# A SwiGLU layer on one core: the first loads of a kernel move between three issuing queues

## The chip, the core and the metric

The kernel runs on one core of one Trainium2 chip. A core has TensorE (PE in the profile, its weight loads PEld), VectorE (DVE), ScalarE (ACT), GpSimd (POOL) and SyncE (SP). SP does no arithmetic; it issues DMAs. The metric is the device time of one execution in microseconds (us); of the kernel before there are three runs. A profile of one more execution gives a span, from the first to the last instruction, and the times of all instructions and DMAs, counted here from the start of the span.

## What is computed

x has 2048 tokens of 512 values, and the hidden width F is 1376 (10 tiles of 128 columns and one of 96); all inputs are bf16.

```python
g = silu(x @ w_gate)      # x: 1 x 2048 x 512, w_gate: 512 x 1376
u = x @ w_up              # w_up: 512 x 1376
out = (g * u) @ w_down    # w_down: 1376 x 512
```

## The kernel before

TensorE works through a list of groups written out in the program (`groups`). A group G or U is 128 columns of F (a tile `ft`) of the gate or up product for 512 tokens (a chunk `c`): four steps over the depth of 512 (`dk`), each of two matmuls of 64 columns of F that run side by side in the array, into one of eight PSUM banks. ScalarE takes the silu of a gate out of its bank, VectorE multiplies it by the up product into `hT_sb`. After four chunks of this, and of the 96 columns that are left (groups X and Y), the same array computes the output from `hT_sb` and w_down in groups of four 32-row strips (`strips`, L456) and at the end in whole rows (`whole_rows`, L433). TensorE waits for a load the first time that it uses it (`need`).

The contraction runs over x's depth, so x is needed with depth on partitions (`xT_sb`). Tokens 256 and up are transposed by DMA (`load_x`, L93). The first 256 tokens come as they are into `xn_sb` (L114), and TensorE transposes them with an identity matrix (L374, L382), which GpSimd's iota (L274) and VectorE (L299) make; VectorE and ScalarE copy the result into `xT_sb` (L309, L291). Until `xn` has landed, TensorE runs matmuls on constants whose results nobody reads: `N_WARM` of 512 columns (L359), and `N_FILL` pairs of 128 columns with half the rows each (L364).

The order of the first useful work is written out by hand at L385 to L394: for tiles 0 and 1, gates and ups of tokens 0 to 255 (32 matmuls of 256 columns), then tile 0's gate of tokens 256 to 383 and of 384 to 511 (8 matmuls of 128 columns each), then the other three groups of tokens 256 to 511 (24 matmuls of 256 columns). The next groups are the gates of tiles 2 and 3 and their ups, with 512 tokens at once, and so on.

The loads that the change touches, with the name of each one's semaphore:

- `xn`: tokens 0 to 255; `x0b` and `x0c`: tokens 256 to 383 and 384 to 511, transposed.
- `wg0`, `wu0`: gate and up weights of tiles 0 and 1 (256 KB each); `wg2`, `wu2`: of tiles 2 and 3; `wg4`, `wu4` and so on in the same way (`slabs`).

Each engine's DMA instructions go through that engine in program order. Before, `wg0` is the first instruction of ScalarE (`loads_on_scalar`, L110). All the others are SP's (`loads_on_sync`, L113): xn, wu0, x0b, x0c, wg2, wu2, wg4, wu4 and on. GpSimd issues no DMA.

Of the kernel before, what the change touches and what calls it, by code (L numbers as in the profile page):

```python
# [6 lines left out]
BF16 = mybir.dt.bfloat16  # L7
FP32 = mybir.dt.float32

N_WARM = 6  # L10
N_FILL = 2


def bass_standalone__swiglu_ffn__prompt_kernel(nc, x, w_gate, w_up, w_down, out):
    _, S, D = x.shape
    F = w_gate.shape[1]
    P = 128
# [24 lines left out]
    UPH = F + 32  # L42
# [4 lines left out]
    with ExitStack() as es:  # L47
# [33 lines left out]
        loads = {}  # L81

        def load_sem(name):
            loads[name] = sem(f"s_{name}")
            return loads[name]
# [6 lines left out]
        def load_x(eng, name, t0, t1):  # L92
            eng.dma_start_transpose(  # L93
                xT_sb[:, :, t0:t1], xf[t0:t1, :]
            ).then_inc(load_sem(name), 16)

        def load_w(eng, name, src, base, f0, f1):
            eng.dma_start(
                w_sb[:, :, base + f0:base + f1],
                src[:, f0:f1].rearrange("(k p) f -> p k f", p=P),  # L100
            ).then_inc(load_sem(name), 16)

        slabs = [(0, 2), (2, 4), (4, 6), (6, 8), (8, NFT)]
        slab_of = {ft: a for a, b in slabs for ft in range(a, b)}

        def load_slab(eng, a, b):
            load_w(eng, f"wg{a}", w_gate, 0, a * P, min(b * P, F))
            load_w(eng, f"wu{a}", w_up, UPH, a * P, min(b * P, F - 32))

        def loads_on_scalar(act):  # L110
            load_w(act, "wg0", w_gate, 0, 0, slabs[0][1] * P)

        def loads_on_sync(sp):  # L113
            sp.dma_start(  # L114
                xn_sb[:, :, :].rearrange("p j d -> p (j d)"), xf[0:HT, :].rearrange("(p j) d -> p (j d)", j=NXN)
            ).then_inc(load_sem("xn"), 16)
            load_w(sp, "wu0", w_up, UPH, 0, slabs[0][1] * P)
            load_x(sp, "x0b", HT, HT + P)
            load_x(sp, "x0c", HT + P, SC)
            for a, b in slabs[1:]:  # L120
                load_slab(sp, a, b)
            load_w(sp, "wut", w_up, F - (F - 32), F - 32, F)
            for c in range(1, NSC):
                load_x(sp, f"x{c}", c * SC, (c + 1) * SC)
            sp.dma_start(
                wd_sb[:, 0:NFF, :], w_down[0:NFF * P, :].rearrange("(k p) d -> p k d", p=P)
            ).then_inc(load_sem("wd"), 16)
            for c in range(NSC):
                sp.dma_start(
                    wdt_sb[R * c:R * (c + 1), :, :], w_down[NFF * P:F, :].rearrange("(q p) d -> p q d", p=R)  # L130
                ).then_inc(load_sem(f"wdt{c}"), 16)
            sp.dma_start(wdl_sb[:, :], w_down[NFF * P:F, LASTA:D]).then_inc(load_sem("wdl"), 16)
# [86 lines left out]
        for dk in range(KD):  # L219
            g = add_group("T", dk=dk)  # L220
            eng = "DA"[dk % 2]
# [19 lines left out]
        for at in range(NST):  # L241
# [4 lines left out]
            for c0, c1 in [(0, LASTA), (LASTA, LASTB), (LASTB, D)] if end else [(0, D)]:  # L246
                g = add_group("O", t=t, c0=c0, c1=c1, c=c)
                (quads[j] if c0 == 0 else last).append(g)
                eng = "A" if (end and c0 == 0) or (j < TPC - 1 and c % 2) else "D"
                op = add_op(  # L250
                    eng, g, kind="copy", out=o_sb[ob][:, c0:c1], src=g["bank"][:, 0:c1 - c0],
# [6 lines left out]
        def rows_of(t):  # L258
            if t < NXN:
                return of[0:HT, :].rearrange("(p j) d -> j p d", j=NXN)[t]  # L260
            return of[t * P:(t + 1) * P, :]

        def on_sync(sp):
            loads_on_sync(sp)
            for t, c0, c1, ob, eng, n in stores:
                if (c0, c1) == (0, LASTA):
                    continue
                sp.wait_ge(s_A if eng == "A" else s_D, n)
                sp.dma_start(rows_of(t)[:, c0:c1], o_sb[ob][:, c0:c1]).then_inc(s_out[ob], 16)
            for i in range(NST, NST + NOS):  # L270
                sp.wait_ge(s_out[i % NOS], 16 * n_store[i % NOS])

        def on_gpsimd(pool):
            pool.iota(  # L274
                diag[:, :], pattern=[[-1, P]], base=0, channel_multiplier=1,
            ).then_inc(s_I, 1)

        def on_scalar(act):
            loads_on_scalar(act)
            act.activation(adummy[:, 0:4], zero_c, ACT.Silu)  # L280
            for op in act_ops:
                act.wait_ge(s_P, op["g"]["at"] + 1)
                if op["kind"] == "silu":
                    if op["free"]:
                        act.wait_ge(s_D, op["free"])
                    fn = ACT.Silu
                else:
                    if op["stored"][1]:
                        act.wait_ge(*op["stored"])
                    fn = ACT.Copy  # L290
                act.activation(op["out"], op["src"], fn).then_inc(s_A, 1)  # L291
            for t, c0, c1, ob, eng, n in stores:
                if (c0, c1) == (0, LASTA):
                    act.wait_ge(s_A, n)
                    act.dma_start(rows_of(t)[:, c0:c1], o_sb[ob][:, c0:c1]).then_inc(s_out[ob], 16)
# [16 lines left out]
        def on_tensor(pe):  # L312
# [44 lines left out]
            def warm(n, width):  # L357
                for i in range(n):
                    pe.matmul(banks[NB - 1][:, 0:width], lhsT=ones_w, rhs=ones_m[:, 0:width], start=True, stop=True)  # L359

            warm(N_WARM, SC)
            for i in range(N_FILL):
                for h in range(2):
# [147 lines left out]
                ).then_inc(s_P, 1)  # L511

        on_sync(nc.sync)
        on_gpsimd(nc.gpsimd)
        on_scalar(nc.scalar)
        on_tensor(nc.tensor)
        on_vector(nc.vector)

# [27 lines left out]
```

## Time and profile before

| What | us |
|---|---|
| runs (three) | 120.25, 119.51, 119.60; median 119.6 |
| profiled execution | 120.67 |
| its span | 119.3 |
| PE busy | 116.6 (98%) |
| DVE, ACT busy | 43.4, 35.5 |
| POOL busy | 0.4 |
| matmuls of L345 (gate and up) | 71.0 in 680 |
| matmuls of L456, L433 (output) | 26.9 in 480, 8.7 in 59 |

The profiled execution is 1.37 us longer than its span, and 1.07 us longer than the median of the runs. The records of a few matmuls are missing from a trace like this. "Idle" of TensorE can be hidden in its busy time, since the ends of matmuls are modelled; the starts are measured.

### The profile page before, as it was taken

How to read it: one execution, taken by the hardware profiler on the slowest of the kernel's cores; microseconds unless marked ns; L12 is line 12 of the kernel's file. 1: busy time of each engine (PE TensorE's matmuls, PEld its weight loads, DVE VectorE, ACT ScalarE, POOL GpSimd, SP SyncE). 2: the span in 40 equal slices, each digit the busy share in tenths (PEclk: the TensorE clock that was granted, in tenths of full speed). 3: DMA queues.
4: the chain of work that ended last, by engine and by line, in shares of the span. 5: the costliest groups of instructions: out<-in, count | busy, mean ns of one | idle time of the engine just before them, and what ended most of it. 6: DMA issues, size and time to landing. Idle time of an engine off the chain costs nothing.

```text
span 119.3 us, 2992 instructions
## 1 busy us (share of the span) xinstructions
PE 116.6 (98%) x1343; PEld 66.4 (56%) x1344; DVE 43.4 (36%) x68; ACT 35.5 (30%) x61; POOL 0.4 (0%) x5
## 2 busy tenths in 40 slices
PE   7999999999999999999999999999999999999993
PEld 2796555555555555555555555554444444464452
DVE  0103534442534452444352444369800040214331
ACT  4225243265242365232454323470000030213001
POOL 1000000000000000000000000000000000000000
DMA  3999999991000000000000000000000023023612
GB/s 80 278 283 335 194 253 228 269 295 23 0 5 0 0 0 0 5 0 5 0 5 0 0 0 0 5 0 0 5 0 5 0 86 95 0 92 106 204 44 88
DMA packets 17596, 8.92 MB, mean 75 GB/s; under 512 B 8624, under 2 KB 17456, under 8 KB 17584
## 3 DMA queue, kind: packets, MB, share of 16 engines
q1 hardware_dynamic: 16912, 8.38, 27.1%
q10 hardware_dynamic: 672, 0.36, 1.0%
q8 instruction: 10, 0.16, 0.6%
q14 instruction: 2, 0.02, 0.0%
HBM read 4.81 MB, written 2.10 MB: 58 GB/s over the span
## 4 chain that ended last, share of the span: by engine, by line
PE 98%; issue 0%; DVE 0%
PE psum L345 59%; PE psum L456 24%; PE psum L433 7%; PE psum L409 3%; PE psum L359 2%; PE psum L420 1%; PE psum L382 0%; PE psum L374 0%; PE psum L364 0%; DVE o_sb L309 0%; PE psum L508 0%
## 5 line engine op out<-in xcount | busy, mean ns | idle before, releaser
L345 PE MATMUL psum<-xT_sb,w_sb 128*64 128x512 bf16 (+2 forms) x680 | 71.0, 371 | 0.0
L345 PEld LDWEIGHTS psum<-xT_sb,w_sb 128*64 128x64 bf16 x680 | 43.0, 112 | 27.1
L305 DVE TENSOR_TENSOR hT_sb<-sg_sb,psum 128x512 bf16<-128x512 f32 x40 | 27.5, 687 | 41.5 <-PE psum L345 36.6
L291 ACT ACTIVATE sg_sb<-psum 128x512 f32<-128x512 f32 x40 | 23.8, 596 | 41.6 <-PE psum L345 41.6
L456 PE MATMUL psum<-wd_sb,hT_sb 32*128 32x512 bf16 x480 | 26.9, 374 | 0.0
L456 PEld LDWEIGHTS psum<-wd_sb,hT_sb 32*128 32x128 bf16 x480 | 13.0, 93 | 13.0 <-issue 0.4
L309 DVE CAST o_sb<-psum 128x512 bf16<-128x512 f32 (+1 forms) x11 | 6.4, 603 | 25.2 <-PE psum L456 19.9
L291 ACT ACTIVATE o_sb<-psum 128x512 bf16<-128x512 f32 (+1 forms) x7 | 3.7, 580 | 33.0 <-PE psum L456 25.9
L433 PE MATMUL psum<-wd_sb,hT_sb 128*128 128x512 bf16 (+2 forms) x59 | 8.7, 307 | 0.2 <-issue 0.2
L433 PEld LDWEIGHTS psum<-wd_sb,hT_sb 128*128 128x128 bf16 x60 | 4.6, 98 | 4.6 <-issue 0.4
L305 DVE TENSOR_TENSOR ht_sb<-sgy_sb,yu_sb 32x512 bf16<-32x512 f32 x8 | 5.5, 683 | 0.4
L409 PE MATMUL psum<-xT_sb,w_sb 128*64 128x512 bf16 x32 | 4.2, 379 | 0.0
L305 DVE TENSOR_TENSOR ht_sb<-sgx_sb,psum 32x512 bf16<-32x512 f32 x4 | 2.8, 691 | 3.5 <-ACT sgx_sb L291 3.5
L291 ACT ACTIVATE sgx_sb<-psum 32x512 f32<-32x512 f32 x4 | 2.4, 588 | 4.5 <-PE psum L409 4.5
L359 PE MATMUL psum<-const-bfloat16-1.0 128*128 128x512 bf16 x6 | 2.7, 623 | 0.8 <-PEq L531 0.8
L456 PE MATMUL psum<-wdt_sb,ht_sb 32*128 32x512 bf16 (+1 forms) x48 | 3.3, 371 | 0.0
L409 PEld LDWEIGHTS psum<-xT_sb,w_sb 128*64 128x64 bf16 x32 | 2.0, 110 | 1.4
L291 ACT ACTIVATE sgy_sb<-psum 64x512 f32<-64x512 f32 x4 | 2.4, 590 | 0.1
L456 PEld LDWEIGHTS psum<-wdt_sb,ht_sb 32*128 32x128 bf16 x48 | 1.3, 93 | 1.3
L420 PE MATMUL psum<-xT_sb,w_sb 128*64 128x512 bf16 x16 | 1.9, 379 | 0.0
L359 PEld LDWEIGHTS psum<-const-bfloat16-1.0 128*128 128x128 bf16 x6 | 0.7, 133 | 1.9 <-issue 1.9
L280 ACT ACT_TABLE_LOAD x1 | 1.3, 1283 | 1.2 <-PEq L531 1.2
(21 smaller groups left out, 7.6 us busy)
## 6 DMA issues: line engine op xcount, KB each, us to landing
out_dram<-o_sb SPq DMA_DIRECT2D x15, 128.0 KB, 1.8
wd_sb<-in_w_down_dram SPq DMA_DIRECT2D x1, 1280.0 KB, 8.9
w_sb<-in_w_up_dram SPq DMA_DIRECT2D x4, 256.0 KB, 4.0
w_sb<-in_w_gate_dram SPq DMA_DIRECT2D x3, 256.0 KB, 3.9
wdt_sb<-in_w_down_dram SPq DMA_DIRECT2D x4, 96.0 KB, 7.2
w_sb<-in_w_gate_dram SPq DMA_DIRECT2D x1, 352.0 KB, 6.2
w_sb<-in_w_up_dram SPq DMA_DIRECT2D x1, 320.0 KB, 6.3
w_sb<-in_w_gate_dram ACTq DMA_DIRECT2D x1, 256.0 KB, 3.6
```

Source lines behind the costliest of these rows:

```text
L280: act.activation(adummy[:, 0:4], zero_c, ACT.Silu)
L291: act.activation(op["out"], op["src"], fn).then_inc(s_A, 1)
L305: ins = dve.tensor_tensor(op["out"], op["a"], op["b"], ALU.mult)
L309: ins = dve.tensor_copy(op["out"], op["src"])
L345: ins = pe.matmul(g["bank"][m:m + HC, n0:n1], lhsT=w_sb[:, dk, col + m:col + m + HC], rhs=xT_sb[:, dk, c * SC + n0:c * SC + n1], start=(dk ...
L359: pe.matmul(banks[NB - 1][:, 0:width], lhsT=ones_w, rhs=ones_m[:, 0:width], start=True, stop=True)
L409: ins = pe.matmul(g["bank"][m:m + HC, :], lhsT=w_sb[:, dk, XC0 + m:XC0 + m + HC], rhs=xT_sb[:, dk, c * SC:(c + 1) * SC], start=(dk == 0), ...
L420: ins = pe.matmul(g["bank"][y0:y1, :], lhsT=w_sb[:, dk, YC0:YC0 + 64], rhs=xT_sb[:, dk, c * SC:(c + 1) * SC], start=(dk == 0), stop=(dk == ...
L433: ins = pe.matmul(g["bank"][:, 0:c1 - c0], lhsT=hT_sb[:, fk, t * P:(t + 1) * P], rhs=wd_sb[:, fk, c0:c1], start=(start and fk == 0), stop= ...
L456: ins = pe.matmul(g["bank"][:, 0:c1 - c0], lhsT=h(r, g["t"]), rhs=w[R * r:R * (r + 1), c0:c1], start=(start and n == 0), stop=final, tile_ ...
```

## The change

SP issues `xn`, then `wg0`, `wu0`, `x0b`, `x0c`, then `wu2` and the other weights as before, without `wg2`. ScalarE issues no load. GpSimd, after its iota, waits until `wg0` has landed and then issues `wg2`. The matmuls on constants become five of 512 columns and four pairs of 128 columns (before: six, and two pairs). The order in which the engines' programs are written down changes, not what is in them. TensorE's, VectorE's and ScalarE's arithmetic is the same in the same order.

```diff
-N_WARM = 6
-N_FILL = 2
+N_WARM = 5
+N_FILL = 4
...
-        def load_slab(eng, a, b):
-            load_w(eng, f"wg{a}", w_gate, 0, a * P, min(b * P, F))
+        def load_slab(eng, a, b, gate=True):
+            if gate:
+                load_w(eng, f"wg{a}", w_gate, 0, a * P, min(b * P, F))
             load_w(eng, f"wu{a}", w_up, UPH, a * P, min(b * P, F - 32))
-
-        def loads_on_scalar(act):
-            load_w(act, "wg0", w_gate, 0, 0, slabs[0][1] * P)
 
         def loads_on_sync(sp):
             sp.dma_start(
                 xn_sb[:, :, :].rearrange("p j d -> p (j d)"), xf[0:HT, :].rearrange("(p j) d -> p (j d)", j=NXN)
             ).then_inc(load_sem("xn"), 16)
-            load_w(sp, "wu0", w_up, UPH, 0, slabs[0][1] * P)
+            load_slab(sp, *slabs[0])
             load_x(sp, "x0b", HT, HT + P)
             load_x(sp, "x0c", HT + P, SC)
             for a, b in slabs[1:]:
-                load_slab(sp, a, b)
+                load_slab(sp, a, b, gate=a != slabs[1][0])
...
             pool.iota(
                 diag[:, :], pattern=[[-1, P]], base=0, channel_multiplier=1,
             ).then_inc(s_I, 1)
+            pool.wait_ge(loads["wg0"], 16)
+            load_w(pool, "wg2", w_gate, 0, slabs[1][0] * P, slabs[1][1] * P)
 
         def on_scalar(act):
-            loads_on_scalar(act)
             act.activation(adummy[:, 0:4], zero_c, ACT.Silu)
```

More of the change, by code (lines that the diff above doesn't have):

```diff
@@ L513, in bass_standalone__swiglu_ffn__prompt_kernel @@
         on_sync(nc.sync)
+        on_scalar(nc.scalar)
         on_gpsimd(nc.gpsimd)
-        on_scalar(nc.scalar)
         on_tensor(nc.tensor)
```

## The prediction

> **What bounds the kernel now.** I read the page's chain first, then the same chain in order of time, then the loads of the first 10 us, because the diff touches nothing else.
>
> The page's chain, the chain in order of time (start us, length us, what):
>
> ```profile
> PE 98%; issue 0%; DVE 0%
> ...
> 0.77 2.72 PE psum L359 x6
> 3.49 0.33 PE psum L364 x3
> 3.82 0.33 PE psum L374 x11
> 4.15 0.36 PE psum L382 x4
> 4.51 18.56 PE psum L345 x200
> ```
>
> TensorE carries the whole span: placeholder matmuls (L359, L364), the transposes of x (L374, L382), then useful matmuls (L345) without a hole to the last output. So the end moves only if the transposes start at another time, if a load comes too late for L345, or if the matmuls change their pace. The transposes need `xn`. The starts of SP's issues, and the loads' times from issue to landing (rows of the DMA view, asked for stretch by stretch):
>
> ```profile
> 0.74 0.41 SPq L114 DMA_DIRECT2D xn_sb<-in_x_dram  x1
> 1.20 0.41 SPq L98 DMA_DIRECT2D w_sb<-in_w_up_dram  x1
> 1.67 2.57 SPq L93 DMA_TRANSPOSE xT_sb<-in_x_dram  x2
> 4.28 0.58 SPq L98 DMA_DIRECT2D w_sb<-in_w_gate_dram  x1
> 4.91 0.51 SPq L98 DMA_DIRECT2D w_sb<-in_w_up_dram  x1
> ...
> w_sb<-in_w_gate_dram ACTq DMA_DIRECT2D x1, 256.0 KB, 3.6
> xn_sb<-in_x_dram SPq DMA_DIRECT2D x1, 256.0 KB, 2.9
> ...
> w_sb<-in_w_up_dram SPq DMA_DIRECT2D x1, 256.0 KB, 4.0
> xT_sb<-in_x_dram SPq DMA_TRANSPOSE x1, 4.1
> ...
> xT_sb<-in_x_dram SPq DMA_TRANSPOSE x1, 3.2
> ...
> w_sb<-in_w_gate_dram SPq DMA_DIRECT2D x1, 256.0 KB, 3.5
> ```
>
> Issue plus landing: `xn` 0.74 + 2.9 = 3.6; `wg0` (ScalarE, 0.73) 4.3; `wu0` 5.2; `x0b` 1.67 + 4.1 = 5.8; `x0c` (the second of the two transposes in its line, issued at 2.97 to 4.23) 2.97 + 3.2 = 6.2; `wg2` 4.28 + 3.5 = 7.8; `wu2` 4.91 + 3.7 = 8.6.
>
> The needs follow from the matmuls' pace, which is not constant (starts of the first and last, then in the same form for later):
>
> ```profile
> L345 PE MATMUL psum<-xT_sb,w_sb x18: 393/421/423, 4.4 to 6.1; 128*64 128x256 bf16 x18
> ...
> L345 PE MATMUL psum<-xT_sb,w_sb x22: 272/273/273, 7.8 to 8.9; 128*64 128x256 bf16 x22
> ```
>
> 18 matmuls of 256 columns start within 1.7 us (0.1 us each, in pairs 0.213 apart), later 22 within 1.1 us (0.054 each, pairs 0.109 apart). The first 64 units of 256 columns run from 4.42 to 9.07, where the first 512-column matmul, which needs `wg2`, starts. With h units at 0.107 and the others at 0.0545, 0.0525 h = 4.65 - 3.49, so h = 22 and the pace doubles at 4.42 + 22 x 0.107 = 6.8. So the needs are: `wg0` 4.4, `wu0` 5.9, `x0b` 7.2, `x0c` 7.5, `wg2` 9.0 (its weight load), `wu2` 10.6. Slack: 0.1, 0.7, 1.4, 1.3, 1.1 and 2.0 us. Were the pace full from the first, 16 units would end at 5.3, 32 at 6.2, 36 at 6.4 and 64 at 7.9, with slack of 0.1, 0.4, 0.2 and 0.1 for the same loads. That matters, since the profiled execution took 120.67 us (span 119.3) and the runs 119.51 to 120.25: a doubling 2.1 us earlier, at 4.7, would by itself take 2.1 / 2 = 1.07 us off and give the median of 119.6. This is an estimate; the trace has one execution.
>
> **The change, part by part.**
>
> *Placeholders.* One L359 goes (starts 0.43 apart: 6 in 2.56 us plus the last) and four more L364 come (two pairs took 3.42 to 3.63, so two pairs more 0.21). TensorE reaches the transposes at 3.63 - 0.43 + 0.21 = 3.41 and not 3.63. They can't start before `xn` lands. `xn` is still SP's first issue at 0.74, and nothing of ScalarE's queue is beside it any more. In the slices this was little:
>
> ```profile
> 2.00:2.50 0.50, 0.50 (x3) 0.21 (x2) 0.00 (x0) 0.50 (x1) 0.00 (x0) 1.00 0.65 143
> 2.50:3.00 0.50, 0.50 (x3) 0.08 (x1) 0.00 (x0) 0.22 (x2) 0.00 (x0) 1.00 0.74 266
> 3.00:3.50 0.50, 0.50 (x4) 0.08 (x4) 0.00 (x0) 0.00 (x0) 0.00 (x0) 1.00 1.08 337
> 5.50:6.00 0.50, 0.50 (x8) 0.50 (x6) 0.00 (x0) 0.00 (x0) 0.00 (x0) 1.00 0.74 84
> ```
>
> (Half a microsecond each: busy time of the five engines, then PEclk, the DMA share and GB/s.) Until 3.0 the engines aren't full, so `wg0` took little from `xn`; only after that is the rate at its 340 GB/s. Landing between 3.4 and 3.6; I take 3.5, a start 0.1 us earlier.
>
> *`wg0` on SP.* It now takes the place that `wu0` had, issue at 1.20 instead of 0.73. Lower bound: bytes. `xn` and `wg0` are 512 KB; before, the stream had also moved part of `wu0` when `wg0` landed at 4.3, so it may land at 4.1. Upper bound: the whole 0.47 us later, 4.8. The middle is 4.45 to 4.5; I take 4.5. The first L345 would then start at 4.56 instead of 4.42: +0.14 us, bounds -0.2 (start 4.21) and +0.45. If the doubling of the pace stays where it is, a shift ahead of it costs half, because what is moved behind it runs twice as fast: +0.07, bounds -0.1 and +0.23. ScalarE loses its 0.46 us issue, ahead of a table load that it has 3 us for: nothing.
>
> *`wu0`, `x0b`, `x0c`.* Each is issued 0.47 later. `wu0` is held by bytes: `xn`, `wg0` and `wu0` end as before, at about 5.2, at worst at 5.7 for a need of 5.9. `x0c`'s issue ends at 4.70 and not 4.23, so it lands at 6.2 to 6.65 for a need of 7.5. Nothing here, in the profiled execution. With a full pace from 4.7 the need is some 6.6: a stall of 0 to 0.1, and 0.3 at most if the pace is full from 4.4.
>
> *SP's queue behind.* Past the first three it is 0.47 later, without `wg2` 0.62 earlier: `wu2` and all after it 0.16 us earlier, with slack anyway. SP's later issues and the stores are not touched otherwise.
>
> *`wg2` from GpSimd.* The instruction waits for `wg0`. GpSimd has nothing else queued after it (its last work was the iota at 0.82), so nobody waits behind it but TensorE's gates of tiles 2 and 3. No row shows a DMA issued by GpSimd. The nearest are SP's and ScalarE's of the same 256 KB: 3.5 to 4.4 us from issue to landing. From 4.55 that is 8.05 to 8.95, for a need of 9.0. Below this nothing is likely, since `x0c` and `wu2` share the engines. On the other side stands SP's transposing issue: 1.26 us for 128 tokens where a plain one takes 0.58, so 0.7 us more, 9.65 at the upper end: a stall of 0.6 us. The farthest row, the transpose of 512 tokens (issue 4.8 us, landing after 7.0), would give 11.5 and a stall of 2.5. I take 8.5: no stall, and no cost. The Trainium skill ("DMA: Bandwidth & Descriptors", Rules for kernel authors) says that spreading DMAs over engines doesn't help bandwidth and only saves issue time, which speaks against this part. By its fit for GpSimd's path (Anatomy of one DMA), 2.0 us and the bytes at 436 GB/s, an estimate is 2.6 us and a landing at 7.2; no run here shows it yet.
>
> The sum, against the profiled execution's own 120.67: -0.05 (start) + 0.12 (`wg0`) + 0 = +0.07 us. On the median of the runs that gives 119.7.
>
> **The rivals.**
>
> *Nothing is late* (start at 3.41, `wg0` at 4.1 to 4.2): -0.2 us of start, -0.1 if half of it counts. 119.4 to 119.5. For it: less traffic beside `xn`. Against: the engines weren't full while `xn` came.
>
> *GpSimd's gates come too late.* At 9.0 TensorE stops until `wg2` lands. It decides from a landing at 9.0, or some 8.0 where the pace doubles early. With the landing at 8.95 and the early doubling the stall is 0.95 us, with 9.65 and the late one 0.65: 120.3 to 120.6. Both upper ends together, 9.65 against 8.0, give 121.3. For it: the issue waits for a landing that itself moves later, and the gates share the DMA engines with `x0c`, `wu2` and `wg4`. Against: the rows of SP's loads, which share them too and land within 4.4.
>
> *The doubling is put off.* If TensorE stands idle before the transposes and before `wg0` and the pace doubles only after a stretch of unbroken work, the price is half of the delay. If the half pace lasts after a hole ending at 4.5 as long as it lasted from 0.77 (6.0 us), it ends at 10.5 and not 6.8: 3.7 / 2 = +1.9 us, 121.5. It decides from the first idle stretch longer than those of before (0.1 us between L374 and L382 and again ahead of L345). The Trainium skill ("TensorE: Matmul & The Clock Gate", Part 1) has such a rule: half clock until one busy window of about 3.4 us, windows running freely, so that one lost window costs 3.4 / 2 = 1.7 us. The trace agrees in the two paces, while PEclk shows 1.00 throughout.
>
> *The start doesn't move* (`xn` at 3.6 as before, TensorE only waits where it used to compute placeholders): 119.6.
>
> **How the numbers follow.** Forecast (+0.07, 119.7 with 119.5 to 120.1 around it) 0.45; nothing late 0.25; late gates 0.15; put-off doubling 0.08; start unmoved 0.07. Low end: the -0.2 in full and the lowest run, 119.2. High end: 120.9, midway between the late gates' 120.6 and the 121.3 for which both upper ends must meet; beyond it are the put-off doubling and the far transposing row. About 1% (1.2 us, twice the runs' spread of 0.7) is what a measurement can tell. Slower by more than that is the put-off doubling and a part of the late gates, 0.14; faster has no mechanism but an earlier doubling, 0.02.
>
> **What would show it.** In the changed profile: L374 starting at 3.4 to 3.65; L345 at 4.2 to 4.9 with `wg0`'s landing just ahead; the place where 421 ns matmuls turn into 273; GpSimd's row with its time to landing; a hole, or none, ahead of the first 512-column matmul. I am wrong if that hole is over 0.3 us, or if the pace doubles in another place.

## The result and the profile after

The changed kernel takes 120.88 us (median of 11 runs, 120.36 to 121.51), the kernel before 119.73 (11 runs, 119.50 to 120.55). The ratio is 1.0088, 95% interval 1.0065 to 1.0111: slower by nearly 1%. The profiled execution took 120.77 us, its span 119.5. Medians and ranges here and below are of all runs of a kernel; ratios and intervals leave out those more than 1.5% above its shortest (three of nine without the wait, one of four with GpSimd behind `xn`, two of four with the transposes on ScalarE).

The chain of the changed kernel, first by engine, then in order of time (start us, length us, what):

```profile
PE 91%; DMA 6%; issue 0%; SPq 0%; DVE 0%
...
1.21 3.24 DMA w_sb<-in_w_gate_dram
4.45 0.29 issue
4.74 4.38 DMA w_sb<-in_w_gate_dram
9.12 0.04 issue
9.16 14.00 PE psum L344 x128
```

Before, TensorE alone carried the chain (98%). Now it runs through two loads: the first gates (`wg0`), issued by SP at 1.21 and landed at 4.45; then 0.29 us until GpSimd issues; then the gates of tiles 2 and 3 (`wg2`), landed at 9.12; and only then the first 512-column matmul, which had been waiting for them. The waits of TensorE's weight loads (us in total, times, the longest):

```profile
PEld psum L344 <- DMA w_sb<-in_w_gate_dram: 0.8, 2, 0.5
...
PEld psum L373 <- DMA xn_sb<-in_x_dram: 0.2, 1, 0.2
```

The two waits for gates are 0.3 us ahead of the first useful matmul and 0.5 us ahead of the gates of tiles 2 and 3. Neither was there before. The issues of GpSimd and SP:

```profile
4.74 0.87 POOL L98 DMA_DIRECT2D w_sb<-in_w_gate_dram  x1 [3.67 <-DMA w_sb<-in_w_gate_dram]
...
0.75 0.40 SPq L112 DMA_DIRECT2D xn_sb<-in_x_dram  x1
1.21 0.42 SPq L98 DMA_DIRECT2D w_sb<-in_w_gate_dram  x1
1.68 0.50 SPq L98 DMA_DIRECT2D w_sb<-in_w_up_dram  x1
2.22 2.57 SPq L93 DMA_TRANSPOSE xT_sb<-in_x_dram  x2
4.83 0.58 SPq L98 DMA_DIRECT2D w_sb<-in_w_up_dram  x1
```

The loads from issue to landing, from the DMA view by stretches: `xn` 2.7, `wg0` 3.2, `wg2` 4.4, `x0c` 2.8:

```profile
xn_sb<-in_x_dram SPq DMA_DIRECT2D x1, 256.0 KB, 2.7
w_sb<-in_w_gate_dram SPq DMA_DIRECT2D x1, 256.0 KB, 3.2
...
w_sb<-in_w_gate_dram POOLq DMA_DIRECT2D x1, 256.0 KB, 4.4
xT_sb<-in_x_dram SPq DMA_TRANSPOSE x1, 2.8
```

And the pace of L344, in two stretches, as in the prediction:

```profile
L344 PE MATMUL psum<-xT_sb,w_sb x12: 421/421/422, 4.5 to 5.6; 128*64 128x256 bf16 x12
...
L344 PE MATMUL psum<-xT_sb,w_sb x16: 272/273/344, 6.0 to 6.8; 128*64 128x256 bf16 x16
```

By the starts of single matmuls it doubles at 6.2 here and at 6.8 in the trace before. That difference is why the two profiled executions are nearly as long as each other (120.77 and 120.67), while the medians are 1.15 us apart: the execution that was profiled before was among the longest of its kernel, with a late doubling. In all traces of this study the time is 97.6 to 97.7 us plus the moment when the gate and up matmuls of the first chunk end (in the chains: 4.51 + 18.56 = 23.07 before, 9.16 + 14.00 = 23.16 after). Only the first 23 to 24 us differ (26.6 in one trace), and the last 14.0 of them are the same 128 matmuls, so the time is 111.6 us plus the start of the first 512-column matmul. By the same sum, as an estimate, the median before (119.73) belongs to a first 512-column matmul at 8.1, the median after (120.88) to one at 9.3.

### The profile page after: what moved, and what is told of

Read it like the earlier page. It is cut to its first block, busy times and chain, and to the rows that moved or that the text cites. A ratio compares the mean times of both kernels' runs of the same rounds, so it can differ in the third digit from the quotient of the medians.

```text
span 119.5 us, 2999 instructions
## 1 busy us (share of the span) xinstructions
PE 116.5 (98%) x1347; PEld 61.2 (51%) x1347; DVE 43.4 (36%) x68; ACT 35.5 (30%) x61; POOL 1.3 (1%) x6
## 4 chain that ended last, share of the span: by engine, by line
PE 91%; DMA 6%; issue 0%; SPq 0%; DVE 0%
PE psum L344 55%; PE psum L455 24%; PE psum L432 7%; DMA w_sb<-in_w_gate_dram 6%; PE psum L408 3%; PE psum L419 1%; SPq L112 0%; DVE o_sb L308 0%; PE psum L507 0%
## 5 line engine op out<-in xcount | busy, mean ns | idle before, releaser
L344 PE MATMUL psum<-xT_sb,w_sb 128*64 128x512 bf16 (+2 forms) x680 | 70.8, 370 | 0.3 <-DMA w_sb<-in_w_gate_dram 0.2
L344 PEld LDWEIGHTS psum<-xT_sb,w_sb 128*64 128x64 bf16 x680 | 38.4, 112 | 31.9 <-DMA w_sb<-in_w_gate_dram 0.8
L408 PEld LDWEIGHTS psum<-xT_sb,w_sb 128*64 128x64 bf16 x32 | 1.8, 110 | 1.6
L308 DVE COPY xT_sb<-psum 128x256 bf16<-128x256 bf16 x2 | 0.5, 292 | 2.5 <-PE psum L373 2.5
```

The costliest lines, as they stand in the source:

```text
L308: ins = dve.tensor_copy(op["out"], op["src"])
L344: ins = pe.matmul(g["bank"][m:m + HC, n0:n1], lhsT=w_sb[:, dk, col + m:col + m + HC], rhs=xT_sb[:, dk, c * SC + n0:c * SC + n1], start=(dk ...
L408: ins = pe.matmul(g["bank"][m:m + HC, :], lhsT=w_sb[:, dk, XC0 + m:XC0 + m + HC], rhs=xT_sb[:, dk, c * SC:(c + 1) * SC], start=(dk == 0), ...
```

## Experiments: which part costs it

**The gates of tiles 2 and 3 back on SP.** From the changed kernel:

```diff
-                load_slab(sp, a, b, gate=a != slabs[1][0])
+                load_slab(sp, a, b)
...
-            pool.wait_ge(loads["wg0"], 16)
-            load_w(pool, "wg2", w_gate, 0, slabs[1][0] * P, slabs[1][1] * P)
```

> The changed kernel with the gates of tiles 2, 3 issued by SP again, between x0c and the ups; placeholders and the first gates on SP stay as changed. Theory A (the gates of tiles 2, 3 come too late through GpSimd, and that alone costs the time): SP issues them at about 4.8 and they land 3.5 us later, 8.3, so the hole ahead of the first 512-column matmul goes; 119.6 to 120.0, ratio to the kernel before 0.998 to 1.003. Theory B (the new order at the start costs it: the first gates 0.47 us later, fewer placeholders): still 120.6 to 121.0, ratio 1.007 to 1.011.

Measured: 120.15 us (10 runs, 119.95 to 120.47), ratio 1.0012, interval 0.9986 to 1.0038. The chain has TensorE alone again, and the load takes 3.3 us from issue to landing:

```profile
4.38 17.94 PE psum L342 x200
...
w_sb<-in_w_gate_dram SPq DMA_DIRECT2D x1, 256.0 KB, 3.3
```

The new start (placeholders, `wg0` on SP) can't be told from the old one. What the change costs goes with GpSimd's load. What is left of theory B is at most 0.4%: the shortest of these runs, 119.95, is longer than the shortest before, 119.48, which would fit `x0c` landing at 6.7 here and at 6.2 before, or `wg2` landing at 8.1 here and at 7.8 and 7.4 in the two traces of the kernel before. Neither was tested by itself.

**GpSimd's load alone**, in the kernel before: the same GpSimd lines behind its iota, SP without `wg2`, ScalarE still issuing `wg0`.

```diff
-                load_slab(sp, a, b)
+                load_slab(sp, a, b, gate=a != slabs[1][0])
...
+            pool.wait_ge(loads["wg0"], 16)
+            load_w(pool, "wg2", w_gate, 0, slabs[1][0] * P, slabs[1][1] * P)
```

> The kernel before with one edit: the gates of tiles 2, 3 go from SP to GpSimd behind the landing of the first gates, which ScalarE still issues. Theory A: first gates land at 4.3, GpSimd issues at 4.6, its load takes 4.4 us, 9.0, and TensorE stands still ahead of the first 512-column matmul; 120.6 to 120.9, ratio 1.006 to 1.010. Theory B: no hole that counts, 119.6 to 119.9, ratio 0.998 to 1.002.

Measured: 121.22 us (6 runs, 120.75 to 121.41), ratio 1.0108, interval 1.0076 to 1.0141. Theory A holds, somewhat above its range. The chain and the wait:

```profile
4.68 4.85 DMA w_sb<-in_w_gate_dram
9.52 0.04 issue
9.57 14.00 PE psum L348 x128
...
PEld psum L348 <- DMA w_sb<-in_w_gate_dram: 1.7, 1, 1.7
```

In this execution the pace had doubled before the first useful matmul at 4.47, so TensorE was through with all that it had by 8.0 and stood still for over 1.5 us. The early doubling, which makes the kernel before short, gains nothing here: the landing at 9.5 sets the time.

**Only the placeholders**, in the kernel before:

```diff
-N_WARM = 6
-N_FILL = 2
+N_WARM = 5
+N_FILL = 4
```

> The kernel before with the changed placeholders alone (five of 512 columns, four pairs of 128). Here and in the traces so far, the time is 111.6 us plus the start of the first 512-column matmul (before 9.07 and 120.67, changed 9.16 and 120.77). TensorE is ready 0.2 us earlier than xn can land (3.6) and waits; nothing else moves: 119.6 to 120.2, ratio 0.997 to 1.003. If the placeholders that are gone put the doubling of the pace off, it is 0.3 to 1.7 us slower, ratio 1.003 to 1.014.

Measured: 120.13 us (10 runs, 119.51 to 120.67), ratio 1.0013, interval 0.9978 to 1.0047: no difference that can be told. The transposes start at 3.65, as before, because `xn` lands at 3.6 as before.

## Experiments: is it the wait, or GpSimd's way of loading

**Without the wait.** From the changed kernel:

```diff
-            pool.wait_ge(loads["wg0"], 16)
```

> The changed kernel without GpSimd's wait: it issues the gates of tiles 2, 3 right behind its iota, at about 1.1. Theory A: with 4.4 us to landing they are there at 5.5 to 6.5 and the hole goes; what is left is how much their bytes delay the first gates and ups, 0 to 0.5 us of start at half price or full: 119.6 to 120.2, ratio 0.999 to 1.004. Theory B: 120.6 or more, since the start is at least as late as in the changed kernel.

Measured: 121.19 us (9 runs, 120.34 to 123.19), ratio 1.0079, interval 1.0040 to 1.0118. Theory A's expectation was missed, and theory B was not the reason: the gates of tiles 2 and 3, issued at 1.34, land at 6.5, early enough, but the ups of tiles 0 and 1 come late. The chain and the wait:

```profile
1.67 4.97 DMA w_sb<-in_w_up_dram
6.64 0.04 issue
6.68 16.63 PE psum L343 x184
...
PEld psum L343 <- DMA w_sb<-in_w_up_dram: 0.8, 1, 0.8
```

With the gates of tiles 2 and 3 on SP the same load of ups took 4.0 us (landing at 5.6). Take the wait away, and GpSimd's load delays another that is needed first.

**The same wait, but ScalarE issues.** From the changed kernel, without GpSimd's lines:

```diff
-            for op in act_ops:
+            for i, op in enumerate(act_ops):
+                if i == 2:
+                    act.wait_ge(loads["wg0"], 16)
+                    load_w(act, "wg2", w_gate, 0, slabs[1][0] * P, slabs[1][1] * P)
```

> The changed kernel with the gates of tiles 2, 3 issued by ScalarE instead of GpSimd, behind the same landing of the first gates and behind ScalarE's two copies into xT_sb, so at about 4.85, when GpSimd issued them at 4.74. It tells the wait apart from GpSimd's way of issuing. If the wait alone makes them late: landing still near 9.1, ratio 1.007 to 1.010. If GpSimd's path is what is slow: landing 3.5 us after the issue, 8.3 to 8.5, and 119.7 to 120.2, ratio 1.000 to 1.004.

Measured: 120.91 us (10 runs, 120.40 to 121.28), ratio 1.0074, interval 1.0047 to 1.0102. By the ratio the wait alone would be to blame, but the trace shows that neither reading is right. ScalarE issued at 4.27, and the gates landed 3.2 us later, at 7.5, early enough; what stopped TensorE was `x0c`:

```profile
3.52 4.17 DMA xT_sb<-in_x_dram
7.68 0.04 issue
7.73 15.54 PE psum L345 x160
...
w_sb<-in_w_gate_dram ACTq DMA_DIRECT2D x1, 256.0 KB, 3.2
...
PEld psum L345 <- DMA xT_sb<-in_x_dram: 1.4, 1, 1.4
```

`x0c` took 4.2 us, against 2.8 to 3.3 in the traces of the kernels before, changed, with the gates on SP and with GpSimd's load alone, where no other queue moved packets between 4.1 us and its landing. So a load through GpSimd takes longer (4.4 and 4.85 us, against 3.2 from ScalarE, 3.3 from SP in the kernel with the gates on SP, and 3.1 to 3.9 from SP over the five traces in which SP issues it and no other queue moves packets meanwhile), and a second queue can hold up a load that SP has in flight.

The packets of the changed kernel tell where GpSimd's time goes. The first line is from 6.0 to 7.0, the others are from 7.4 to 8.7 (queue, kind: packets, MB, share of the engines' time; q0 is GpSimd's, q1 SP's):

```profile
q1 hardware_dynamic: 132, 0.07, 55.7%
...
q0 software_dynamic: 80, 0.26, 56.4%
q1 hardware_dynamic: 400, 0.20, 50.5%
```

GpSimd issued at 4.74, but its first packet moves only at 7.48, 2.7 us later (1.9 to 3.1 in the five traces with a load of GpSimd's); ScalarE's came 1.1 us behind its issue here. From 6.0 to 7.0 SP's queue, alone, moved only 0.07 MB. Once GpSimd's packets move, all 80 do so within 1.2 us. So most of this load's length is the time before its first packet, and other loads' bytes don't explain all of it. What does is open.

**GpSimd behind `xn` instead of `wg0`.** From the changed kernel:

```diff
-            pool.wait_ge(loads["wg0"], 16)
+            pool.wait_ge(loads["xn"], 16)
```

> The changed kernel with GpSimd waiting for xn (landing 3.5) instead of the first gates (4.45). The issue moves about 0.95 us ahead, to 3.8. If the landing follows the issue by 4.4 to 4.85 us as in the changed kernel and with GpSimd's gates alone: 8.2 to 8.7, the first 512-column matmul there or a little behind, 119.9 to 120.5, ratio 1.000 to 1.005. If the bytes then hold up the loads that are needed ahead of it (ups of tiles 0, 1 or tokens 256 to 511), as without any wait: 120.5 or more, with a hole ahead of those.

Measured: 122.16 us (4 runs, 121.16 to 124.24), ratio 1.0155, interval 1.0081 to 1.0228. It is the second reading of the expectation. Issued at 3.8, GpSimd's load fell together with the two transposing loads; it took 5.9 us itself, and `x0c` 6.1:

```profile
3.52 6.08 DMA xT_sb<-in_x_dram
9.61 0.04 issue
9.65 16.98 PE psum L344 x160
...
PEld psum L344 <- DMA xT_sb<-in_x_dram: 2.7, 2, 1.7
```

From 6.0 to 8.0 GpSimd's and SP's queues together moved 0.10 MB, where SP's alone moved 0.43 with the gates on SP. So these loads weren't just waiting for other loads' bytes; what held them up is open.

The traced execution is the longest of the four, and 124.24 - 26.63 (end of the first chunk's matmuls) is 97.6 all the same. But the holes are not all that it has more. The pace had doubled at 5.8. From 7.0 to 9.65 TensorE ran only eight matmuls, and behind that it is at half pace again. First a row by stretches (PEclk is the third figure from the end), then the matmuls from 9.6 to 12.3:

```profile
9.65:10.50 0.85, 0.85 (x12) 0.80 (x14) 0.00 (x0) 0.17 (x1) 0.00 (x0) 0.50 1.15 346
...
L344 PE MATMUL psum<-xT_sb,w_sb x30: 313/421/421, 9.7 to 12.2; 128*64 128x256 bf16 x22, 128*64 128x128 bf16 x8
```

The matmuls from tile 0's gate of tokens 384 to 511 up to the first one of 512 columns take 2.99 us here (9.65 to 12.64), and 1.56 with the gates on ScalarE (7.73 to 9.29): 1.4 us are the half pace that came back. It is what brings the mean granted clock of this execution to 0.986; the other three have 1.000 and took 121.16 to 122.56.

**GpSimd issues another load.** If lateness were all, a load that is needed late would cost nothing. From the changed kernel, `wg4` goes to GpSimd and `wg2` stays on SP:

```diff
-                load_slab(sp, a, b, gate=a != slabs[1][0])
+                load_slab(sp, a, b, gate=a != slabs[2][0])
...
-            load_w(pool, "wg2", w_gate, 0, slabs[1][0] * P, slabs[1][1] * P)
+            load_w(pool, "wg4", w_gate, 0, slabs[2][0] * P, slabs[2][1] * P)
```

> The changed kernel with GpSimd issuing the gates of tiles 4, 5 instead of those of tiles 2, 3, behind the same wait; SP issues the gates of tiles 2, 3 where GpSimd's load is left out now. GpSimd's load is needed only after four more tiles' worth of matmuls, at 11.6 or later, and lands near 9.1 to 9.6. Theory A (only what comes through GpSimd late and is needed early costs): as with the gates back on SP, 119.9 to 120.4, ratio 1.000 to 1.004. If a GpSimd load in flight by itself holds up the others or TensorE: 120.6 or more.

Measured: 120.98 us (10 runs, 120.17 to 121.72), ratio 1.0080, interval 1.0048 to 1.0111. Theory A falls in the form that it had. SP's own `wg2`, issued at 4.84 as with the gates on SP, now takes 4.5 us and not 3.3, and TensorE waits for it:

```profile
4.84 4.47 DMA w_sb<-in_w_gate_dram
9.32 0.04 issue
9.36 14.01 PE psum L344 x128
...
PEld psum L344 <- DMA w_sb<-in_w_gate_dram: 0.9, 2, 0.7
```

What the DMA engines did from 7.2 to 8.2 (queue, kind: packets, MB, share of the engines' time), here and, in the second fence, with the gates on SP:

```profile
q0 software_dynamic: 52, 0.19, 65.0%
q1 hardware_dynamic: 171, 0.09, 29.3%
```

```profile
q1 hardware_dynamic: 604, 0.30, 108.3%
```

SP's queue (q1) moved 0.09 MB in that microsecond and not 0.30. GpSimd's load comes in 4096-byte packets (0.19 MB in 52, with 4-byte ones among them), SP's weights in 512-byte ones. The Trainium skill ("DMA: Bandwidth & Descriptors", Queues, rings and completion order) says that a DMA engine takes turns between queues packet by packet. The trace agrees in direction: if each packet is a turn, 4096 against 512 bytes gives GpSimd the larger part, and it has 0.19 to 0.09. That the size is the cause is not shown. ScalarE's load moves in 512-byte packets like SP's, and `x0c` landed late beside it too (4.2 us).

So the theory that stands has two halves. GpSimd's load is slow itself (4.4 to 5.9 us); and while its packets move SP's loads get less: 0.09 MB for 0.30 in the microsecond above, and 0.12 in the changed kernel from 7.4 to 8.4. Whichever is needed first stops TensorE. In the changed kernel it is the first half: SP's loads in flight from 7.4 on are `wu2` (landed at 8.4, needed at 10.7) and `wg4`, which have slack, and `wg2` has none.

## Experiments: the pace, and a try at a faster version

**No placeholders at all**, in the kernel before:

```diff
-N_WARM = 6
-N_FILL = 2
+N_WARM = 0
+N_FILL = 0
```

> The kernel before without any placeholder matmul; TensorE stands still until xn lands at 3.6. It prices the half pace. If the pace doubles a fixed stretch of work after TensorE's start (0.77 with placeholders, doubling seen between 4.3 or earlier and 6.8, so 3.5 to 6.0 us of work), it doubles here at 7.1 to 9.7; by first 512-column matmul = 7.91 + 0.49 x (doubling - 4.42) that starts at 9.2 to 10.5, so 120.8 to 122.1, ratio 1.008 to 1.019. If the doubling has nothing to do with the placeholders, 119.6 to 120.7 as before.

Measured: 121.10 us (8 runs, 120.55 to 121.56), ratio 1.0091, interval 1.0058 to 1.0125. In the trace the pace doubles at 8.6, some 4.9 us after the transposes' start at 3.66, and the 200 matmuls of L345 take 19.40 us, where the two traces of the kernel before have 18.56 and 18.44:

```profile
0.74 2.88 DMA xn_sb<-in_x_dram
3.62 0.05 issue
3.66 0.50 PE psum L374 x11
4.16 0.35 PE psum L382 x4
4.52 19.40 PE psum L345 x200
```

The placeholders are worth 1.3 us at the medians (121.10 against 119.77). In the traces it is 0.8 to 1.0, and all of it is the doubling: useful matmuls start at 4.4 in all three.

**The kernel before, one more trace.**

> The kernel before unchanged, one more trace. If the pace of the matmuls doubles at a moment of its own in every execution, this trace has another moment than 6.8 and its time is 111.6 us plus the start of the first 512-column matmul; if the doubling is tied to the work, it comes at 6.8 again and the time is 120.7.

Measured: 120.57 us. The doubling comes at 6.5, the first 512-column matmul starts at 8.97, and 111.6 + 8.97 = 120.57. The chain's row is the counterpart of the 18.56 us of the profile before:

```profile
4.53 18.44 PE psum L345 x200
```

In the eleven traces with placeholders the doubling came at 3.7 (ScalarE issuing behind `wg0`), 5.0, 5.4, 5.8, 5.9, 6.2, 6.2, 6.5 and 6.8, and in two between the last transposes at 4.1 and the first useful matmul at 4.5 and 5.0. The mean granted clock is 1.000 in all but that of GpSimd behind `xn`. So the doubling moves by 3 us from trace to trace, at half price. How much of that the ten kernels' different starts cause is not shown; one and the same kernel has 6.5 and 6.8. A doubling that moves fits the kernel before, whose runs go from 119.5 to 120.6: its shortest, less 111.6, gives a first 512-column matmul at 7.9, which is the 64 units at full pace from 4.42. The Trainium skill ("TensorE: Matmul & The Clock Gate", Part 1) has the doubling after one busy window of about 3.4 us, and the windows run freely. An estimate by that is between 4.2 and 7.6 for work that starts at 0.77, and between 7.1 and 10.5 without placeholders. The traces agree but for the 3.7, which comes 2.9 us after the first matmul and so less than one window.

**The two transposing loads on ScalarE**, from the kernel with the gates on SP: both placed behind ScalarE's first activation, and SP waits for them before its later transposes. ScalarE's program is also written down ahead of SP's. It was the try at landing everything early.

```diff
-            load_x(sp, "x0b", HT, HT + P)
-            load_x(sp, "x0c", HT + P, SC)
...
+            sp.wait_ge(loads["x0b"], 16)
+            sp.wait_ge(loads["x0c"], 16)
             for c in range(1, NSC):
...
             act.activation(adummy[:, 0:4], zero_c, ACT.Silu)
+            load_x(act, "x0b", HT, HT + P)
+            load_x(act, "x0c", HT + P, SC)
```

> The kernel with the gates back on SP, and the two transposing loads of tokens 256 to 511 issued by ScalarE behind its table load instead of by SP (SP waits for both before its later transposes). It is the try at a version ahead of both kernels: xn lands at 3.5 as with the gates on SP, and SP's weights are issued 2.6 us earlier. If the issue time on SP is all that counts, every load is ahead of its need even at the early doubling, 119.4 to 119.9, ratio 0.995 to 1.001. If a transposing load lands late whenever another queue's bytes are in flight beside it (7.7 with the gates on ScalarE, 9.6 with GpSimd behind xn, against 6.2 to 6.7 otherwise): a hole ahead of the matmuls on tokens 256 to 511, 120.4 or more.

Measured: 123.14 us (4 runs, 121.66 to 124.08), ratio 1.0169, interval 1.0105 to 1.0233. The second reading: `x0c`, issued at 2.12, lands 6.3 us later, at 8.5, behind SP's weights; `wu0` takes 5.4 us. No kernel tried here is faster than the one before.

## Why the prediction was right and where it was wrong

The measured 120.88 is inside the range (119.2 to 120.9), by 0.02 us, and the change is under the 1% that the prediction took as what a measurement can tell. That it lies inside is luck: the upper end was put midway between two prices of a rival. The forecast itself, 119.7, was 1.2 us short, and the case that came true is that rival, the late gates, which had 0.15. The prediction's own sign of being wrong came too: the weight loads' hole ahead of the first 512-column matmul is 0.5 us, over the 0.3 that it set. Its other sign, a doubling in another place, tells nothing, since the kernel before moves it by itself (6.8 and 6.5).

*The start: right.* `xn` landed at 3.5 (taken: 3.5), `wg0` at 4.45 (4.5), the first L344 began at 4.50 (4.56), `x0c` landed at 6.3 (6.2 to 6.65), `wu2` landed 0.17 us earlier than before (0.16), though it was issued only 0.08 earlier. With the gates on SP all of this together gave a ratio of 1.0012. Of the rivals, "Nothing is late" failed on `wg2`; "The start doesn't move" failed by 0.1 us, 3.54 for 3.65, which no time shows.

*"I take 8.5: no stall, and no cost": wrong.* This is the step that failed, in three terms. GpSimd began 0.29 us after the landing and not 0.05. From issue to landing it took 4.4, the upper end of SP's rows, where I had taken the middle (and 4.85 with GpSimd's load alone). That gives 9.12. And the need was put at 9.0, from the profiled execution, although the same text had worked out that the median run doubles its pace earlier and needs the gates at about 8.0. The median before of 119.73 gives 8.1. Adding +0.07 from an execution with a late doubling to a median with an early one left the stall out: with my own 8.5 against 8.0 the sum would have been 0.5 us, with the measured start at 9.16 against 8.1 it is 1.0, and the medians are 1.15 apart.

*The price of the late gates has the same mix.* For a landing at 9.65 and the late doubling the text added a stall of 0.65 to the early median, 120.3. But a late landing sets the time by itself: 111.6 and 9.7 give 121.3 at either pace, and the 8.95 gives 120.6. The span of this rival was 120.6 to 121.3, and the 120.88 lies in it.

*"the rows of SP's loads, which share them too and land within 4.4", named against the late gates: a false comfort.* Those rows are SP's own queue, its loads issued one behind another. With a second queue in flight other kernels here showed loads of 5 to 6 us.

*The put-off doubling didn't happen*, though TensorE now waits 0.2 us for `xn` and 0.3 for `wg0`: 6.2 against 6.8 and 6.5 before. Its price, half of the delay, was shown with no placeholders: the doubling 1.8 us later than in the first trace of the kernel before, the first 512-column matmul 0.85 later (9.92 for 9.07). That a stop brings the half pace back was seen once, behind the long one in the trace of GpSimd behind `xn`.

*The Trainium skill's rule against spreading DMAs* ("DMA: Bandwidth & Descriptors", Rules for kernel authors) pointed the right way. The Trainium skill's fit for GpSimd's path ("DMA: Bandwidth & Descriptors", Anatomy of one DMA) gave an estimate of 2.6 us and a landing at 7.2. Measured were 4.4 us and 9.1.

## What to carry to other kernels

A load that is moved to a second queue is priced twice: by its own time from issue to landing on that queue, and by what it does to the loads in flight beside it. A need that depends on something that changes from execution to execution (here the moment at which the first matmuls double their pace) must be taken as the median run has it, and the profiled execution's place among the runs tells whether its trace is a usual one. A load that is issued behind another's landing costs both loads' times: here the second one landed at 9.1 and, with GpSimd's load alone, at 9.5, and TensorE's pace, which doubled late in the one and early in the other, made no difference to that.

## What the runs showed of the hardware that I had not expected

- A 256 KB load issued by GpSimd took 4.4 to 5.9 us to land (five traces), 1.9 to 3.1 of them ahead of its first packet and 0.87 the issue; the gates of tiles 2 and 3 from ScalarE took 3.2, and from SP, with its queue alone, 3.1 to 3.9. It moved in 4096-byte packets, SP's and ScalarE's weights in 512-byte ones. Beside it SP's queue moved 0.09 MB in a microsecond, and 0.30 without it.
- The transposing load `x0c` (128 tokens, 128 KB) landed after 2.8 to 3.3 us where no other queue moved packets behind 4.1 us, after 4.2 beside ScalarE's load, and after 4.0 and 6.1 beside GpSimd's (without the wait, and behind `xn`). Why is open: it was not tried with loads of other sizes.
- The moment at which matmuls double their pace moved between 3.7 and 6.8 us from trace to trace, with PEclk at 1.00 on both sides of it in the traces of before and after.
- After 2.7 us with only eight matmuls, TensorE ran at half pace again for 2.8 us, this time with PEclk at 0.50 (one trace).
